# Attention feeding two expert stages: 128 partitions hold two token groups of one head instead of two heads

## The chip, the cores and the metric

The kernel runs on one core of one Trainium2 chip. The metric is the device time of one execution in microseconds. Engines are called as in the profile: PE (TensorE, with its weight loads as PEld), ACT (ScalarE), DVE (VectorE), POOL (GpSimd) and SP (SyncE), which issues the DMAs here.

## What is computed

```python
kv = np.einsum('bhsd,bhse->bhde', k, v)          # batch 4, heads 8, tokens 576, head size 64
out = np.einsum('bhsd,bhde->bhse', q, kv)
rms = np.sqrt(np.mean(out * out, axis=-1, keepdims=True) + 1e-06)
x = (out / rms * g_norm)                          # regrouped to 2304 tokens x 512
h = x @ w_in                                      # first expert stage, d_ff 2048
x = (h * np.clip(h + 3.0, 0.0, 6.0) / 6.0) @ w_out
p = domain_probs / (domain_probs.sum(-1, keepdims=True) + 1e-09)
for e in range(4):                                # second expert stage, 1024 wide each
    out += p[:, e:e + 1] * (np.maximum(x @ w1[e], 0.0) @ w2[e])
```

All inputs and the output are float32.

## The kernel before

The program has three stages: linear attention, a feed-forward stage in five units of hidden tiles, and the second expert stage in quads. Only the first is rebuilt by the change, and two small places that follow its token order.

**Head groups.** Attention is worked off in eight head groups i = 0 to 7: batch i // 2, four of the eight heads (HH = 4). The 576 tokens of a head are split as s * 9 + j, with s = 0 to 63 (CP) and j = 0 to 8 (CJ). In SBUF a tile of q, k or v is [128, NP, CJ, D] with NP = 2: partition x * 64 + s, head 2 * r + x. So the two partition halves hold two heads, and a matmul over tokens contracts 64 rows.

**Loads.** `att_load` (line 176) issues one DMA for each of q, k and v. Each writes 128 partitions, in contiguous runs of 9 x 64 floats. The tiles come from six buffers used in turn, so q, k, v of group i + 2 go where those of group i were. All DMAs stand in SP's queue in program order as the scheduler placed it; SP holds the queue while its next DMA waits for a buffer, and each DMA also waits for the landing of the eighth DMA before it (eight semaphores in turn).

**One group on the engines.** The orders of PE, ACT and DVE are written out by hand from line 483 on. For each i: `att_out(i)` multiplies the transposed q with the group's k^T v and squares the result for the norm; `att_q(i + 1)` transposes the next q on PE (line 214 for eight tokens of nine, line 216 for the ninth) and returns the copies to SBUF; `att_rms(i)` computes the scale; `att_kv(i + 1)` (line 225) accumulates k^T v of the next group; then two products of the feed-forward stage's first unit (`ff_mm`, lines 343 to 345), the transposes of the normed result of group i - 1 (`att_x`, line 308), and slices of the conversion of feed-forward weights (`conv`). PE takes them strictly in this order, so `att_kv` holds it until k and v of the next group have landed.

**k^T v before.** The product writes `kvp`, 64 x 64 for each head, two heads above one another:

```python
for j in range(CJ):
    for x in range(2):
        for r in range(NP):
            nc.tensor.matmul(
                kvp[half[x ^ r], r, :D], lhsT=t["k"][half[x], r, j, :], rhs=t["v"][half[x], r, j, :], ...)
```

That is 36 matmuls a group, each with 64 rows and 64 columns. Four neighbours use the four combinations of row half and column half. An f32 matmul leaves two records in the trace, so a group shows 72.

Of the kernel before, what the change touches and what calls it, by code (L numbers as in the profile page):

```python
# [17 lines left out]
def kernel(  # L18
# [18 lines left out]
    nc = tc.nc  # L37
# [136 lines left out]
    natile = [0]  # L174

    def att_load(i):
        b, hf = divmod(i, 2)
        t = {}
        for nm, src in (("q", q), ("k", k), ("v", v)):
            m = natile[0] % 6  # L180
            natile[0] += 1
            pool, tag = (accp, "acc") if m < 5 else (wp, f"w{m - 1}")
            t[nm] = pool.tile([P, NP, CJ, D], F32, tag=tag, name=f"{nm}in")
            nc.sync.dma_start(
                out=t[nm].rearrange("p r j d -> p r (j d)"),
                in_=src[b, hf * HH:(hf + 1) * HH].rearrange("(r x) (s j) d -> (x s) r (j d)", x=2, j=CJ),
            )
        st[i] = t


    half = [slice(x * D, (x + 1) * D) for x in range(2)]
    identx = ident.rearrange("p (x s) -> p x s", x=2)
    GB = TB // D
# [9 lines left out]
    def att_q(i):  # L203

        t = st[i]
        qT = wp.tile([P, (CJ + 1) * P], F32, tag=f"w{i % 2}", name="qT")
        t["qm"] = qm = qT[:, :2 * TB].rearrange("p (r x j s) -> p r x j s", r=NP, x=2, j=CJ // 2)
        t["q8"] = q8 = qT[:D, 2 * TB:].rearrange("p (r x s) -> p r x s", r=NP, x=2)
        pq = [pool.tile([P, 2, CJ // 2, CP], F32, tag=tag, name="pq") for pool, tag in ((psx, "x"), (psa, "a1"))]
        t["kvp"] = kvp = psk.tile([P, NP, TB], F32, tag="k", name="kvp")  # L210
        p8 = kvp[:D, :, D:D + P].rearrange("p r (x s) -> p r x s", x=2)
        for r in range(NP):
            for j in range(CJ // 2):
                nc.tensor.transpose(  # L214
                    pq[r][:, :, j, :], t["q"][:, r, 2 * j:2 * j + 2, :].rearrange("p j d -> p (j d)"), identx)
            nc.tensor.transpose(p8[:, r], t["q"][:, r, CJ - 1, :], identx)
        return [
            lambda r=r: nc.scalar.activation(
                out=qm[:, r].rearrange("p x j s -> p (x j s)"), in_=pq[r].rearrange("p x j s -> p (x j s)"),
                func=AF.Copy)  # L220
            for r in range(NP)] + [
            lambda: nc.scalar.activation(
                out=q8.rearrange("p r x s -> p r (x s)"), in_=kvp[:D, :, D:D + P], func=AF.Copy)]

    def att_kv(i):


        t = st[i]
        kvp = t["kvp"]
        for j in range(CJ):  # L230
            for x in range(2):
                for r in range(NP):
                    nc.tensor.matmul(  # L233
                        kvp[half[x ^ r], r, :D], lhsT=t["k"][half[x], r, j, :], rhs=t["v"][half[x], r, j, :],
                        start=(j == 0), stop=(j == CJ - 1))
        nc.scalar.activation(out=kvd[i % 2][:, 0], in_=kvp[:, :, :D], func=AF.Copy)
        for y in range(2):
            nc.scalar.activation(out=kvd[i % 2][half[y], 1], in_=kvp[half[1 - y], :, :D], func=AF.Copy)
# [3 lines left out]
    def att_out(i):  # L242

        t = st[i]
        kv = kvd[i % 2]
        for jj in range(CJ // 4):
            for r in range(NP):
                for x in range(2):
                    for y, c in ((0, 0), (1, 1), (0, 1), (1, 0)):
                        g = (2 * y + jj) * HH + 2 * r + x  # L250
                        nc.tensor.matmul(
                            group(g)[half[c]], lhsT=t["qm"][half[y], r, x, 2 * jj + c, :],
                            rhs=kv[half[y], x ^ r ^ y, r], start=True, stop=True)
        for x in range(2):
            for r in range(NP):
                g = 2 * GA + x
                nc.tensor.matmul(
                    group(g)[half[r]], lhsT=t["q8"][:, r, x, :], rhs=kv[half[0], x ^ r, r],
                    start=True, stop=True)
# [223 lines left out]
    with tc.manual_schedule(engines=engines):  # L483
# [97 lines left out]
        for y in range(2):  # L581
            h = half[y]
            for jp in range(2):
                j = slice(2 * y + jp, CJ - 1, 4)
                nc.vector.tensor_tensor(
                    out=prob[h, :B * HH].rearrange("p (b a) e -> p b a e", b=B)[:, :, 2 * jp:2 * jp + 2],
                    in0=dp[h, :, j], in1=psum_e[h, :, j].unsqueeze(3).to_broadcast([D, B, 2, E]), op=ALU.mult)
            nc.vector.tensor_tensor(
                out=prob[h, B * HH:], in0=dp[h, y::2, CJ - 1],
                in1=psum_e[h, y::2, CJ - 1:].to_broadcast([D, 2, E]), op=ALU.mult)  # L590

# [149 lines left out]
    def finish(p, e, i, ps):  # L741
# [10 lines left out]
        if e == E - 1:  # L752
            for y in range(2):
                if n < B * HH:
                    b, a = divmod(n, HH)
                    j = 4 * (a % 2) + a // 2 + 2 * y
                else:
                    b, j = 2 * (n - B * HH) + y, CJ - 1
                nc.sync.dma_start(
# [140 lines left out]
```

## Time and profile before

| | us |
|---|---|
| median of 3 runs | 1217.32 |
| lowest, highest | 1217.02, 1217.51 |
| the profiled execution | 1218.32 |
| its span, first to last instruction | 1216.5 |

The profile is that of one execution. Its page gives each engine's busy time, the DMA queues, and the chain of work that ended last. The trace behind it can be cut into stretches, and it says for each wait what ended it. In this profile attention lies in the first 74 us; the feed-forward stage and the second expert stage fill the rest, with PE busy almost throughout. [...]

### The profile page before, as it was taken

What the parts mean: (1) busy time and instruction counts of PE and PEld (TensorE: products, weight loads), DVE (VectorE), ACT (ScalarE), POOL (GpSimd) and SP (SyncE); (2) the same over time, 40 slices, a digit from 0 to 9 for tenths busy, and PEclk for the clock granted to TensorE, in tenths of its full rate; (3) what the DMA queues carried; (4) which work ended last, traced back from release to release, by engine and by line L of the source; (5) the groups of instructions that cost most, each with busy time, mean ns of one, the idle gap of its engine ahead of it and who ended that gap; (6) DMA issues with size and microseconds to landing.
All of it is one profiled execution on the core that took longest, in us unless ns stands there. A gap on an engine that the chain in (4) does not pass through costs nothing.

```text
span 1216.5 us, 17419 instructions
## 1 busy us (share of the span) xinstructions
PE 1195.3 (98%) x6999; PEld 1053.8 (87%) x6999; DVE 770.1 (63%) x1455; ACT 581.7 (48%) x1116; POOL 8.9 (1%) x16
## 2 busy tenths in 40 slices
PE   7899999999999999999999999999999999999997
PEld 6787888888888889999999989999999899999996
DVE  5889999953633844565656585656565856565652
ACT  5766554622322434444444554444445644444441
POOL 2000000000000000000000000000000000000000
PEclk9999999999999999999999999999999999999999
DMA  9612222300200002121111131122221422222202
GB/s 354 223 36 70 87 87 70 95 10 1 70 1 1 1 20 84 70 70 69 69 61 61 62 113 70 70 70 70 70 70 70 121 70 70 70 70 70 70 1 52
DMA packets 59345, 87.18 MB, mean 72 GB/s; under 512 B 3712, under 2 KB 36480, under 8 KB 59264
## 3 DMA queue, kind: packets, MB, share of 16 engines
q1 hardware_dynamic: 59264, 86.07, 21.1%
q8 instruction: 55, 0.90, 0.3%
q14 instruction: 26, 0.21, 0.0%
HBM read 81.34 MB, written 4.72 MB: 71 GB/s over the span
## 4 chain that ended last, share of the span: by engine, by line
PE 93%; DVE 3%; DMA 2%; ACT 1%; issue 1%; SPq 0%; DVEq 0%; ACTq 0%
PE po L734 32%; PE po L378 15%; PE qa L767 14%; PE qb L767 14%; PE ph L343 5%; PE ph L344 5%; PE ph L345 5%; DMA vin<-in_v_dram 1%; DMA qin<-in_q_dram 1%; DVE acc L750 1%; DVE xl L301 1%; PE kvp L233 1%; DVE r L357 0%; PE pq L214 0%; DVE ssq L264 0%
## 5 line engine op out<-in xcount | busy, mean ns | idle before, releaser
L734 PE MATMUL po<-wout,g 128*128 128x512 f32 x1728 | 402.1, 390 | 0.0
L734 PEld LDWEIGHTS po<-wout,g 128*128 128x128 f32 x1728 | 323.6, 188 | 65.4
L767 PE MATMUL qb<-xs,win 128*128 128x384 f32 x1008 | 203.5, 336 | 1.2 <-ACT us L808 1.2
L767 PE MATMUL qa<-xs,win 128*128 128x384 f32 x1008 | 203.1, 336 | 0.0
L378 PE MATMUL po<-gH,w 128*128 128x512 f32 (+1 forms) x632 | 191.8, 368 | 0.0
L767 PEld LDWEIGHTS qb<-xs,win 128*128 128x128 f32 x1008 | 178.1, 188 | 3.8 <-ACT us L808 1.8
L767 PEld LDWEIGHTS qa<-xs,win 128*128 128x128 f32 x1008 | 178.3, 188 | 2.2 <-ACT us L808 0.2
L641 DVE TENSOR_TENSOR wout<-raw,wout 128x512 fp32r<-128x512 f32 x96 | 62.2, 688 | 171.4 <-ACT wout L640 171.4
L640 ACT ACTIVATE wout<-raw 128x512 fp32r<-128x512 f32 x96 | 55.4, 625 | 227.0 <-PE po L734 227.0
L378 PEld LDWEIGHTS po<-gH,w 128*128 128x128 f32 x632 | 115.7, 188 | 20.5 <-ACT acc L392 0.6
L343 PE MATMUL ph<-xh,w 128*128 128x512 f32 (+1 forms) x320 | 119.2, 373 | 1.2 <-DVE r L357 1.2
L344 PE MATMUL ph<-xl,w 128*128 128x512 f32 (+1 forms) x320 | 118.4, 370 | 0.0
L345 PE MATMUL ph<-xh,w 128*128 128x512 f32 (+1 forms) x320 | 118.2, 370 | 0.0
L356 ACT ACTIVATE r<-ph,three 128x512 f32<-128x512 f32 (+1 forms) x80 | 51.6, 645 | 138.3 <-PE ph L345 138.2
L378 PE MATMUL po<-gL,w 128*128 128x512 f32 (+1 forms) x316 | 116.3, 368 | 0.0
L357 DVE SCALAR_TENSOR_TENSOR r<-r,ph 128x512 f32<-128x512 f32 (+1 forms) x80 | 50.5, 631 | 91.0 <-ACT r L356 90.8
L797 DVE SCALAR_TENSOR_TENSOR g<-sums,g 128x384 fp32r<-128x384 f32 x96 | 53.6, 559 | 81.4 <-ACT g L794 81.4
L794 ACT ACTIVATE g<-cs 128x384 fp32r<-128x384 f32 x96 | 50.4, 525 | 63.3 <-DVE cs L810 54.4
L640 ACT ACTIVATE win<-sums 128x512 fp32r<-128x512 f32 x96 | 60.6, 632 | 40.1 <-DVE sums L653 37.6
L343 PEld LDWEIGHTS ph<-xh,w 128*128 128x128 f32 x320 | 60.6, 189 | 12.4 <-DVE r L357 1.6
L797 DVE SCALAR_TENSOR_TENSOR g<-cs,g 128x384 fp32r<-128x384 f32 x96 | 53.2, 554 | 27.2 <-ACT g L794 27.2
L345 PEld LDWEIGHTS ph<-xh,w 128*128 128x128 f32 x320 | 60.6, 189 | 10.3
(129 smaller groups left out, 1260.7 us busy)
## 6 DMA issues: line engine op xcount, KB each, us to landing
raw<-in_moe_w_dram SPq DMA_DIRECT2D x96, 512.0 KB, 4.1
raw<-in_moe_w_in_dram SPq DMA_DIRECT2D x16, 512.0 KB, 3.7
raw<-in_moe_w_out_dram SPq DMA_DIRECT2D x16, 512.0 KB, 3.5
qin<-in_q_dram SPq DMA_DIRECT2D x8, 576.0 KB, 7.1
kin<-in_k_dram SPq DMA_DIRECT2D x8, 576.0 KB, 8.3
vin<-in_v_dram SPq DMA_DIRECT2D x8, 576.0 KB, 9.4
out_dram<-acc SPq DMA_DIRECT2D x36, 128.0 KB, 2.3
dp<-in_moe_domain_probs_dram SPq DMA_DIRECT2D x2, 36.0 KB, 8.4
```

Source lines behind the costliest of these rows:

```text
L343: nc.tensor.matmul(ph, lhsT=w[:, 0, c, :], rhs=xH[t][:, c, :], start=(c == 0), stop=False)
L344: nc.tensor.matmul(ph, lhsT=w[:, 0, c, :], rhs=xL[t][:, c, :], start=False, stop=False)
L345: nc.tensor.matmul(ph, lhsT=w[:, 1, c, :], rhs=xH[t][:, c, :], start=False, stop=(c == KD - 1))
L356: lambda: nc.scalar.activation(out=r, in_=ph, func=AF.Relu, bias=three[:, 0:1]),
L357: lambda: nc.vector.scalar_tensor_tensor(out=r, in0=r, scalar=6.0, in1=ph, op0=ALU.min, op1=ALU.mult),
L378: nc.tensor.matmul(po_t[u, t][o], lhsT=lhsT, rhs=rhs, start=(f == 0 and m == 0), stop=(f == UF[u] - 1 and m == 2))
L640: nc.scalar.activation(out=dst[0], in_=src, func=AF.Copy)
L641: nc.vector.tensor_tensor(out=dst[1], in0=src, in1=dst[0].bitcast(F32), op=ALU.subtract)
L734: nc.tensor.matmul(ps[i], lhsT=lhsT, rhs=w[:, f, y], start=(j == 0 and f == 0 and m == 0), stop=(j == FP - 1 and f == 1 and m == 2))
L767: nc.tensor.matmul(bank, lhsT=w[:, wy, AOP[m], c], rhs=xs[m][:, xy, c], start=first and n == 0, stop=n == 5, skip_group_check=True)
L794: nc.scalar.activation(out=g[f][:, 0, t], in_=src, func=func)
L797: nc.vector.scalar_tensor_tensor(out=g[f][:, 1, t], in0=src, scalar=0.0, in1=g[f][:, 0, t].bitcast(F32), op0=ALU.max, op1=ALU.subtract)
```

## The change

The partition halves hold two groups of tokens of the same head instead of two heads. A tile of q, k or v becomes [128, HH, JG, D] with JG = 5: half y holds tokens j = 5 * y to 5 * y + 4; the second half has four, so the fifth place stays empty there. Each tile is loaded by two DMAs, one for each partition half: 64 partitions with runs of 5 x 64 floats, and 64 partitions with runs of 4 x 64.

k^T v contracts 128 rows for four of the five places and 64 for the fifth: 20 matmuls a group in place of 36. The transposes of q take one head at a time, and those of the ninth token become four of 64 x 64 in place of two of 128 x 64. The output product has the same number and shape of matmuls; its left operand is addressed differently and `kv` loses the swap of heads. Which token stands in which row of the result changes, so the row scales `prob` and the addresses of the output stores follow; their sizes and counts stay.

```diff
@@ -173,6 +173,10 @@
     st = {}
     natile = [0]
 
+    JG, JP = CJ // 2 + 1, CJ // 2
+
+    half = [slice(x * D, (x + 1) * D) for x in range(2)]
+
     def att_load(i):
         b, hf = divmod(i, 2)
         t = {}
@@ -180,16 +184,16 @@
             m = natile[0] % 6
             natile[0] += 1
             pool, tag = (accp, "acc") if m < 5 else (wp, f"w{m - 1}")
-            t[nm] = pool.tile([P, NP, CJ, D], F32, tag=tag, name=f"{nm}in")
-            nc.sync.dma_start(
-                out=t[nm].rearrange("p r j d -> p r (j d)"),
-                in_=src[b, hf * HH:(hf + 1) * HH].rearrange("(r x) (s j) d -> (x s) r (j d)", x=2, j=CJ),
-            )
+            t[nm] = pool.tile([P, HH, JG, D], F32, tag=tag, name=f"{nm}in")
+            for y in range(2):
+                j = slice(y * JG, min((y + 1) * JG, CJ))
+                nc.sync.dma_start(
+                    out=t[nm][half[y], :, :j.stop - j.start].rearrange("p h j d -> p h (j d)"),
+                    in_=src[b, hf * HH:(hf + 1) * HH].rearrange("h (s j) d -> s h j d", j=CJ)[:, :, j]
+                    .rearrange("s h j d -> s h (j d)"))
         st[i] = t
 
 
-    half = [slice(x * D, (x + 1) * D) for x in range(2)]
-    identx = ident.rearrange("p (x s) -> p x s", x=2)
     GB = TB // D
     ppA = psp.tile([P, TB], F32, name="ppA")
     ppB = psp.tile([P, 2 * TB], F32, name="ppB")
@@ -204,35 +208,37 @@
 
         t = st[i]
         qT = wp.tile([P, (CJ + 1) * P], F32, tag=f"w{i % 2}", name="qT")
-        t["qm"] = qm = qT[:, :2 * TB].rearrange("p (r x j s) -> p r x j s", r=NP, x=2, j=CJ // 2)
-        t["q8"] = q8 = qT[:D, 2 * TB:].rearrange("p (r x s) -> p r x s", r=NP, x=2)
-        pq = [pool.tile([P, 2, CJ // 2, CP], F32, tag=tag, name="pq") for pool, tag in ((psx, "x"), (psa, "a1"))]
+        t["qm"] = qm = qT[:, :2 * TB].rearrange("p (h j t) -> p h j t", h=HH, j=JP // 2)
+        t["q8"] = q8 = qT[:D, 2 * TB:].rearrange("p (h s) -> p h s", h=HH)
+        pq = [pool.tile([P, 2, JP // 2, P], F32, tag=tag, name="pq") for pool, tag in ((psx, "x"), (psa, "a1"))]
         t["kvp"] = kvp = psk.tile([P, NP, TB], F32, tag="k", name="kvp")
         p8 = kvp[:D, :, D:D + P].rearrange("p r (x s) -> p r x s", x=2)
-        for r in range(NP):
-            for j in range(CJ // 2):
+        for h in range(HH):
+            r, x = divmod(h, 2)
+            for j in range(JP // 2):
                 nc.tensor.transpose(
-                    pq[r][:, :, j, :], t["q"][:, r, 2 * j:2 * j + 2, :].rearrange("p j d -> p (j d)"), identx)
-            nc.tensor.transpose(p8[:, r], t["q"][:, r, CJ - 1, :], identx)
+                    pq[r][:, x, j, :], t["q"][:, h, 2 * j:2 * j + 2, :].rearrange("p j d -> p (j d)"), ident)
+            nc.tensor.transpose(p8[:, r, x], t["q"][half[0], h, JP, :], ident[half[0], :D])
         return [
             lambda r=r: nc.scalar.activation(
-                out=qm[:, r].rearrange("p x j s -> p (x j s)"), in_=pq[r].rearrange("p x j s -> p (x j s)"),
-                func=AF.Copy)
+                out=qm[:, 2 * r:2 * r + 2].rearrange("p x j t -> p (x j t)"),
+                in_=pq[r].rearrange("p x j t -> p (x j t)"), func=AF.Copy)
             for r in range(NP)] + [
             lambda: nc.scalar.activation(
-                out=q8.rearrange("p r x s -> p r (x s)"), in_=kvp[:D, :, D:D + P], func=AF.Copy)]
+                out=q8.rearrange("p (r x) s -> p r (x s)", x=2), in_=kvp[:D, :, D:D + P], func=AF.Copy)]
 
     def att_kv(i):
 
 
         t = st[i]
         kvp = t["kvp"]
-        for j in range(CJ):
-            for x in range(2):
-                for r in range(NP):
+        for j in range(JG):
+            rows = slice(0, P) if j < JP else half[0]
+            for r in range(NP):
+                for x in range(2):
                     nc.tensor.matmul(
-                        kvp[half[x ^ r], r, :D], lhsT=t["k"][half[x], r, j, :], rhs=t["v"][half[x], r, j, :],
-                        start=(j == 0), stop=(j == CJ - 1))
+                        kvp[half[x], r, :D], lhsT=t["k"][rows, 2 * r + x, j, :], rhs=t["v"][rows, 2 * r + x, j, :],
+                        start=(j == 0), stop=(j == JP))
         nc.scalar.activation(out=kvd[i % 2][:, 0], in_=kvp[:, :, :D], func=AF.Copy)
         for y in range(2):
             nc.scalar.activation(out=kvd[i % 2][half[y], 1], in_=kvp[half[1 - y], :, :D], func=AF.Copy)
@@ -243,19 +249,18 @@
 
         t = st[i]
         kv = kvd[i % 2]
-        for jj in range(CJ // 4):
+        for jj in range(JP // 2):
             for r in range(NP):
                 for x in range(2):
                     for y, c in ((0, 0), (1, 1), (0, 1), (1, 0)):
-                        g = (2 * y + jj) * HH + 2 * r + x
                         nc.tensor.matmul(
-                            group(g)[half[c]], lhsT=t["qm"][half[y], r, x, 2 * jj + c, :],
-                            rhs=kv[half[y], x ^ r ^ y, r], start=True, stop=True)
+                            group((2 * y + jj) * HH + 2 * r + x)[half[c]],
+                            lhsT=t["qm"][half[y], 2 * r + x, jj, half[c]],
+                            rhs=kv[half[y], x ^ y, r], start=True, stop=True)
         for x in range(2):
             for r in range(NP):
-                g = 2 * GA + x
                 nc.tensor.matmul(
-                    group(g)[half[r]], lhsT=t["q8"][:, r, x, :], rhs=kv[half[0], x ^ r, r],
+                    group(2 * GA + x)[half[r]], lhsT=t["q8"][:, 2 * r + x, :], rhs=kv[half[0], x, r],
                     start=True, stop=True)
         t["xt"] = xt = wp.tile([P, NG, D], F32, tag=f"w{2 + i % 2}", name="xt")
         for pt, a, b in PIECES:
@@ -581,13 +586,13 @@
         for y in range(2):
             h = half[y]
             for jp in range(2):
-                j = slice(2 * y + jp, CJ - 1, 4)
+                j = slice(JG * y + jp, JG * y + JP, 2)
                 nc.vector.tensor_tensor(
-                    out=prob[h, :B * HH].rearrange("p (b a) e -> p b a e", b=B)[:, :, 2 * jp:2 * jp + 2],
+                    out=prob[h, :B * HH].rearrange("p (b z a) e -> p b z a e", b=B, z=2)[:, :, jp],
                     in0=dp[h, :, j], in1=psum_e[h, :, j].unsqueeze(3).to_broadcast([D, B, 2, E]), op=ALU.mult)
             nc.vector.tensor_tensor(
-                out=prob[h, B * HH:], in0=dp[h, y::2, CJ - 1],
-                in1=psum_e[h, y::2, CJ - 1:].to_broadcast([D, 2, E]), op=ALU.mult)
+                out=prob[h, B * HH:], in0=dp[h, y::2, JP],
+                in1=psum_e[h, y::2, JP:JP + 1].to_broadcast([D, 2, E]), op=ALU.mult)
 
     N3 = start[NU1 - 1, 0] + 3 * UF[NU1 - 1]
     for n in range(NB, N3 + 1):
@@ -753,9 +758,9 @@
             for y in range(2):
                 if n < B * HH:
                     b, a = divmod(n, HH)
-                    j = 4 * (a % 2) + a // 2 + 2 * y
+                    j = 2 * (a % 2) + a // 2 + JG * y
                 else:
-                    b, j = 2 * (n - B * HH) + y, CJ - 1
+                    b, j = 2 * (n - B * HH) + y, JP
                 nc.sync.dma_start(
                     out=out.rearrange("(b s j) d -> b j s d", b=B, j=CJ)[b, j], in_=acc2[i][half[y]])
```

On SP's queue, the loads of the sixth head group and what follows. Names are tile<-tensor; behind the name stand partitions and elements; the brackets say for what the row waits (DMAHW: a landing). Before:

```order
L184 DMA qin<-in_q_dram 128x2x576 [waits DMAHW5_49,PE_49]
L126 DMA raw<-in_moe_w_in_dram 128x4x256 [waits DMAHW6_49,DVE_49,Activation_49]
L184 DMA kin<-in_k_dram 128x2x576 [waits DMAHW7_49,PE_49]
L184 DMA vin<-in_v_dram 128x2x576 [waits DMAHW0_49]
L499 DMA dp<-in_moe_domain_probs_dram 64x4x36 [waits DMAHW1_49]
L499 DMA dp<-in_moe_domain_probs_dram 64x4x36 [waits DMAHW2_49]
L184 DMA qin<-in_q_dram 128x2x576 [waits DMAHW3_49,PE_49]
L184 DMA kin<-in_k_dram 128x2x576 [waits DMAHW4_49,PE_49]
```

After:

```order
L190 DMA qin<-in_q_dram 64x4x320 [waits DMAHW4_49,PE_49]
L190 DMA qin<-in_q_dram 64x4x256 [waits DMAHW5_49]
L190 DMA kin<-in_k_dram 64x4x320 [waits DMAHW6_49,PE_49]
L190 DMA kin<-in_k_dram 64x4x256 [waits DMAHW7_49]
L190 DMA vin<-in_v_dram 64x4x320 [waits DMAHW0_49]
L190 DMA vin<-in_v_dram 64x4x256 [waits DMAHW1_49]
L126 DMA raw<-in_moe_w_in_dram 128x4x256 [waits DMAHW2_49,DVE_49,Activation_49]
L190 DMA qin<-in_q_dram 64x4x320 [waits DMAHW3_49,PE_49]
L190 DMA qin<-in_q_dram 64x4x256 [waits DMAHW4_49]
L190 DMA kin<-in_k_dram 64x4x320 [waits DMAHW5_49,PE_49]
L190 DMA kin<-in_k_dram 64x4x256 [waits DMAHW6_49]
```

Each load has become two, the third w_in weight load has moved from ahead of the group's k to behind its v, and the two small loads of `dp` are gone from here: they now stand behind the last v.

On PE, from the end of the first group's output product to the second group's k^T v (pq and the part of kvp are the targets of q's transposes). Before:

```order
L214 MATMUL pq<-ident,qin 128x2x64 [waits DMAHW4_49]
L214 MATMUL pq<-ident,qin 128x2x64 x3
L216 MATMUL kvp<-ident,qin 64x128 [waits PE_49]
L214 MATMUL pq<-ident,qin 128x2x64 x4
L216 MATMUL kvp<-ident,qin 64x128
L233 MATMUL kvp<-vin,kin 64x64 [waits DMAHW6_49,DMAHW5_49]
L233 MATMUL kvp<-vin,kin 64x64 x35
```

After:

```order
L219 MATMUL pq<-ident,qin 128x128 [waits DMAHW7_49,DMAHW0_49]
L219 MATMUL pq<-ident,qin 128x128
L221 MATMUL kvp<-ident,qin 64x64 [waits PE_49]
L219 MATMUL pq<-ident,qin 128x128 x2
L221 MATMUL kvp<-ident,qin 64x64
L219 MATMUL pq<-ident,qin 128x128 x2
L221 MATMUL kvp<-ident,qin 64x64
L219 MATMUL pq<-ident,qin 128x128 x2
L221 MATMUL kvp<-ident,qin 64x64
L239 MATMUL kvp<-vin,kin 64x64 [waits DMAHW3_49,DMAHW4_49,DMAHW2_49,DMAHW1_49]
L239 MATMUL kvp<-vin,kin 64x64 x19
```

The ninth token's transposes are four in place of two and stand between pairs of the others. k^T v is 20 matmuls in place of 36, and its first one waits for four landings in place of two. The orders on ACT, DVE and POOL are the same as before.

## Rows read from the trace of the kernel before

**Rows 1.** Head of the page, and its instruction queue: packets, MB, share.

```profile
span 1216.5 us, 17419 instructions
...
PE 1195.3 (98%) x6999; PEld 1053.8 (87%) x6999; DVE 770.1 (63%) x1455; ACT 581.7 (48%) x1116; POOL 8.9 (1%) x16
...
q8 instruction: 55, 0.90, 0.3%
```

**Rows 2.** Stretches: length, busy of PE, PEld, DVE, ACT, POOL; clock, DMA share, GB/s.

```profile
4.00:30.00 26.00, 20.10 (x502) 16.26 (x501) 15.23 (x33) 15.60 (x36) 5.08 (x4) 1.00 1.03 387
...
40.00:62.00 22.00, 20.85 (x458) 17.25 (x461) 17.14 (x36) 16.40 (x39) 2.56 (x2) 0.92 0.54 167
62.00:78.00 16.00, 15.48 (x216) 13.08 (x216) 14.23 (x30) 12.18 (x27) 0.00 (x0) 1.00 0.01 2
...
36.00:46.00 10.00, 7.11 (x156) 5.86 (x156) 5.63 (x13) 5.50 (x13) 0.00 (x0) 0.83 0.79 241
```

**Rows 3.** The chain that ended last, its first part: start us, us, what.

```profile
2.75 8.18 DMA qin<-in_q_dram
10.95 10.83 DMA vin<-in_v_dram
21.91 1.31 PE kvp L233 x72
...
26.30 1.92 issue
...
30.03 1.21 PE kvp L233 x72
...
36.67 1.01 PE kvp L233 x57
37.68 2.89 issue
...
41.85 0.43 PE ph L344
...
49.60 0.24 PE ph L344
...
61.94 1.21 PE kvp L233 x72
...
73.91 1.39 PE po L546 x6
...
92.73 0.70 ACT x L145
```

**Rows 4.** SP's timeline, the last k and v load: start us, us, what.

```profile
49.23 0.37 SPq L184 DMA_DIRECT2D kin<-in_k_dram  x1
49.65 0.46 SPq L184 DMA_DIRECT2D vin<-in_v_dram  x1
```

**Rows 5.** DMA issues of the page: count, KB each, median us to landing.

```profile
vin<-in_v_dram SPq DMA_DIRECT2D x8, 576.0 KB, 9.4
out_dram<-acc SPq DMA_DIRECT2D x36, 128.0 KB, 2.3
```

**Rows 6.** Stretches with output stores (first two) and with loads of expert weights (third).

```profile
709.80:717.50 7.70, 7.12 (x38) 6.47 (x37) 7.63 (x16) 4.29 (x9) 0.00 (x0) 1.00 0.87 203
...
1207.60:1215.30 7.70, 1.41 (x7) 0.83 (x5) 2.20 (x4) 0.00 (x0) 0.00 (x0) 0.76 0.87 203
481.00:484.40 3.40, 3.40 (x21) 3.40 (x20) 2.15 (x5) 2.16 (x6) 0.00 (x0) 1.00 0.87 311
```

**Rows 7.** Matmuls on k and q: xcount, busy us, mean ns, idle before.

```profile
L233 PE MATMUL kvp<-vin,kin 64*64 64x64 f32 x576 | 10.6, 222 | 6.5 <-DMA vin<-in_v_dram 3.6 <-issue 2.9
...
L216 PE MATMUL kvp<-ident,qin 128*64 128x128 f32 x16 | 4.6, 287 | 0.3 <-DVE xl L301 0.2
```

**Rows 8.** What SP's queue waited for: us in total, times, longest us.

```profile
SPq L184 <- PE kvp L216: 13.8, 4, 5.9
SPq L184 <- PE kvp L233: 7.9, 5, 4.0
```

## The prediction

> **What bounds the kernel now.** I first read the head of the page: TensorE is busy for 1195.3 of 1216.5 us [rows 1], so nearly the whole span is the two mixture-of-experts stages, which the change doesn't touch except for a row order in the output. What can move lies in the attention stage. So I next cut the start of the span into stretches [rows 2]. From 4 to 30 us the DMA engines are busy all the time (share 1.03) at 387 GB/s; from 40 to 62 us their share is 0.54; from 62 us it is 0.01. The reader should see two halves there: the first is fed as fast as the queue delivers, the second isn't. Third I read the chain of waits [rows 3]. It begins with a q load that was issued at 2.75 us and landed 8.18 us later, goes on through the v load of the third head group (issued at 10.95, landed at 21.78), and reaches that group's k^T v product at 21.91. After that no load stands in the chain. It has two waits marked "issue", 1.92 us at 26.30 and 2.89 us at 37.68, where TensorE waits for nothing that the profile shows. The last k^T v product, of the eighth group, starts at 61.94, and the first matmul of the feed-forward stage's rest at 73.91. The last v load was issued at 49.65 us [rows 4], long before its product.
>
> So the question is how much slower the loads may become before they set the time again, and how much slower they do become.
>
> **The loads.** Each q, k or v load moves 576 KB (589,824 bytes) [rows 5]. Today one DMA writes it to 128 partitions in rows of 2,304 bytes. After the change two DMAs write 64 partitions each, with rows of 1,280 and 1,024 bytes. No large load to 64 partitions stands in this trace. The nearest rows are the output stores, which move 128 KB each [rows 5] from 64 partitions: of three bursts of twelve the first and the last run at 203 GB/s with the engines 0.87 busy [rows 6]. Their rows have 2,048 bytes. The weight loads of the second expert stage, with rows of 1,024 and 2,048 bytes on 128 partitions, have the same share of 0.87 and reach 311 GB/s [rows 6]. So it isn't the short rows that make the stores slow, and the engines aren't idle during them: their packets take longer. What sets the stores apart is the 64 partitions, and the direction. I take the partitions for the cause, because the share is that of a transfer that is held up and not of one that isn't asked for.
>
> That bounds a load after the change. The slow end is 203 GB/s, 2.91 us. If the gaps of the bursts were filled it would be 203/0.87 = 233 GB/s, 2.53 us. I take the middle, 218 GB/s and 2.71 us, because loads stand close in the queue (share 1.03) but closer packets also meet each other more often. The other bound, were the direction the cause, is 311/0.87 = 357 GB/s, 1.65 us. Today it is 589,824/387 GB/s = 1.52 us.
>
> [...]
>
> **The sum.** The queue works in order. The q load that landed at 10.93 us is its fifth entry, behind three other attention loads and one of 512 KB of weights; the five are 4 x 0.590 + 0.524 = 2.88 MB, or 7.4 us at 387 GB/s, so the queue flows from 10.93 - 7.4 = 3.5 us on. Before the last v load is done it has to move 24 attention loads (14.16 MB) and, in either order, five weight loads of 512 KB (2.62 MB, 6.8 us at 387 GB/s).
> - Before: 3.5 + 14.16 MB/387 + 6.8 = 3.5 + 36.6 + 6.8 = 46.9 us. The last product starts at 61.94, so 15.0 us are spare.
> - After: 3.5 + 14.16 MB/218 + 6.8 = 3.5 + 64.9 + 6.8 = 75.2 us. That is 13.3 us after 61.94.
> - At 203 GB/s: 3.5 + 69.7 + 6.8 = 80.0, 18.1 us later. At 233: 3.5 + 60.8 + 6.8 = 71.1, 9.2 us later.
>
> The loads use up the spare time from about 14.16 MB/(61.9 - 3.5 - 6.8 us) = 274 GB/s. What follows the last product (its copies, the last output product, the norm, the transposes) is one chain on TensorE, ACT and DVE, from 61.94 to 73.91, in the same order as before, so it shifts by the same amount. The second weight half of the third tile is issued behind the last v load; its first reader stands at 92.73 [rows 3] and shifts as well, so nothing waits for it.
>
> The profiled execution took 1218.32 us, its span and 1.8 us around it, 1.0 us above the median of 1217.32. I add the shift to the median: 1217.3 + 13.3 = **1230.6 us**; the profiled execution would become 1231.6.
>
> **The other parts.** The k^T v product goes from 72 records a group to 40 (each f32 matmul leaves two). A group takes 1.21 us, 17 ns a record [rows 3, 7]. Today four records run side by side, one in each quarter of the array; 128 tokens fill both row halves, so two run side by side. By records it would be 40 x 17 ns = 0.67 us, a gain of 0.54; by quarters 20 pairs at 1.21/18 = 67 ns, 1.34 us, a loss of 0.13. I take the loss, since the records overlap (222 ns each at 17 ns distance). Eight groups make between -4.3 and +1.0 us of TensorE time; while each group waits for its v, only the last group's share counts, within 0.6 us either way. The four 64-token transposes in place of two 128-token ones (287 ns a record, overlapping [rows 7]) come to nothing for the same reason. Orders on ACT, DVE and POOL are the same, and copies keep their sizes.
>
> SP issues 24 more DMAs at 0.37 to 0.46 us [rows 4], about 10 us of its time. They cost nothing while a half load occupies the wire for over 1.2 us. Each issue waits for the landing of the eighth DMA before it, now four loads instead of eight. SP waits 13.8 and 7.9 us for TensorE to free q and k buffers [rows 8], and everything behind in the queue waits along. Four loads are 10.8 us of wire, so the queue shouldn't run dry. If it did, a gap costs up to the 2.3 us from issue to landing of an output store [rows 5]; I leave it inside the range.
>
> **Rivals.**
> 1. *The halves run at full rate* (direction was the cause). The last v load would be ready at 3.5 + 14.16 MB/357 + 6.8 = 50 us, out of the way. The third group's v comes 9 x 0.13 = 1.2 us later. Against that, TensorE's stream loses 60 records a group (32 matmuls and as many weight loads, less two transposes with their loads). [...] That makes 1217.3 + 1.2 - 4.8 - 1.2 = 1212.5, **faster**. It decides above 274 GB/s. Chance 0.13. [...]
> 2. *The halves overlap in part*, because some engines fall behind and work on the other half. Near 274 GB/s nothing is left of the loss: **1217**, chance 0.07. Between 274 and 233 GB/s: 1220 to 1226, chance 0.10. For it speaks that DMA engines needn't keep step; against it that the stores also alternate between the halves and still run at 203.
> 3. *The waits lower the clock.* TensorE waits for each v in turn; before, 2.89 us of idleness was followed by the half level, and 1.92 was not. A group now takes 3 x 2.71 = 8.1 us of loads for some 6.6 us of work (the products at 30.03 and 36.67 [rows 3]), so single waits may be long enough. If the last group is caught, its tail pays one or two times 1.2 us: **1232 to 1234**, with 203 GB/s up to 1238. Chance 0.12.
>
> **How the numbers follow.** The forecast has 0.58: 1230.6, by itself 1226.5 to 1235.4. Slower is 0.58 + 0.12 + 0.10 = 0.80; within 0.2% (2.4 us, about what a measurement of this kernel can tell from no change) 0.07; faster 0.13. To hold eight in ten the range leaves out the full-rate rival and reaches from the upper part of the second one to the third with 203 GB/s: 1216 to 1238.
>
> **What would show it.** In the profile of the changed kernel the first 75 us should have a DMA share near 1 at 200 to 240 GB/s; the chain should run through v loads up to the last group, whose product starts near 75 us; waits of TensorE for v should appear in most groups; the "issue" waits should be gone from the chain or hidden. From the last product to the first matmul of the next stage it should be 12 us, as before. I am wrong if the attention loads run above 274 GB/s, or if the last product starts before 66 us.

## The result, and the profile after the change

The changed kernel takes 1231.87 us (median of four runs, 1229.69 to 1233.41) against 1217.41 us for the kernel before: a ratio of 1.0114, with a 95% interval of 1.0096 to 1.0133. The forecast was 1230.6. The profiled execution took 1232.03 us, with a span of 1230.2, 13.7 us longer than before. The total is close to the sum, but terms of the sum are off in opposite directions. The experiments are mostly about two of them, the rate of the loads and the order of the transposes.

The head of the page, to be read against [rows 1]:

```profile
span 1230.2 us, 16980 instructions
...
PE 1206.5 (98%) x6759; PEld 1058.1 (86%) x6759; DVE 769.9 (63%) x1455; ACT 582.3 (47%) x1116; POOL 8.9 (1%) x16
...
q8 instruction: 53, 0.87, 0.3%
```

TensorE has 240 matmul records fewer, the instruction queue moved two packets fewer, and the span is longer all the same. The stretches, as in [rows 2] (length; busy of PE, PEld, DVE, ACT, POOL; clock, which is the share of full speed that TensorE was granted; share of all sixteen DMA engines; GB/s):

```profile
4.00:30.00 26.00, 19.86 (x275) 13.53 (x274) 10.33 (x23) 11.37 (x25) 4.88 (x4) 0.87 1.09 247
30.00:50.00 20.00, 15.76 (x274) 12.18 (x274) 13.90 (x32) 11.92 (x28) 0.18 (x1) 0.91 1.10 249
50.00:70.00 20.00, 19.16 (x323) 15.29 (x324) 12.93 (x28) 12.49 (x30) 2.55 (x2) 0.91 1.10 253
70.00:78.00 8.00, 7.57 (x140) 5.88 (x139) 7.10 (x16) 6.68 (x16) 0.00 (x0) 1.00 0.39 89
```

The engines of the DMA are busy all the time up to 70 us, at 247 to 253 GB/s where [rows 2] has 387. The clock column is below 1 in three stretches: part of each ran at the half level (19.6 to 26.3 us, 33.2 to 36.5 and 50.3 to 53.6, each with a clock of 0.50). The last v load, from the instructions on the tile `vin` between 62 and 80 us (duration of one issue, first and last start; below it the times from issue to landing):

```profile
L190 SPq DMA_DIRECT2D vin<-in_v_dram x2: 596/676/755, 63.2 to 64.1; - x2
...
DMA to landing us min/median/max: 8.9/9.0/9.1
```

Its second half is issued at 64.1 and lands 9.1 us later, at 73.2. Now the chain that ended last, from 38 us on (start us, us, what):

```profile
38.64 11.39 DMA vin<-in_v_dram
...
50.17 2.57 PE kvp L239 x40
...
59.73 1.46 PE kvp L239 x40
...
67.56 1.46 PE kvp L239 x40
...
72.05 1.61 DVE xl L306 x3
...
73.70 0.24 PE kvp L221
73.94 0.37 PE pq L219 x2
74.31 0.17 PE kvp L221
74.49 0.37 PE pq L219 x2
74.86 0.17 PE kvp L221
75.03 0.37 PE pq L219 x2
75.40 0.17 PE kvp L221
75.57 1.46 PE kvp L239 x40
...
87.82 1.39 PE po L551 x6
```

Three things are to be seen. The last product starts at 75.57, close to the 75.2 of the sum, and the next stage's first matmul 12.25 us behind it, as before (11.97). But loads leave the chain at 50.03: the sixth, seventh and eighth group's products follow each other through compute alone, 7.83 and 8.01 us apart (and the sixth 9.56 behind the fifth, which ran at the half level). The last v had been there since 73.2; TensorE reached it 2.35 us late, because after the release of the ninth tokens' bank by DVE's `xl` (it ends at 73.66) four single transposes and six large ones stand ahead of the product, 1.87 us. Before, 0.85 us lay there: two ninth-token transposes and four large ones between 61.09 and 61.94.

So I formed this theory for the experiments: (a) the loads are slow because each DMA reaches one half of the partitions; had the last product followed its v at once, they would have cost 73.2 - 61.9 = 11.3 us; (b) the last 2 us come from TensorE's order of transposes, which the prediction had priced at nothing. The rivals: the loads are slow because of their short rows, their number, or the wait of each issue for the eighth landing before it; and the extra time of the groups comes from k^T v itself.

### The profile page after: what moved, and what is told of

The parts are those of the page before. It is cut to its first block, busy times and chain, and to the rows that moved or that the text cites. A ratio compares the mean times of both kernels' runs of the same rounds, so it can differ in the third digit from the quotient of the medians.

```text
span 1230.2 us, 16980 instructions
## 1 busy us (share of the span) xinstructions
PE 1206.5 (98%) x6759; PEld 1058.1 (86%) x6759; DVE 769.9 (63%) x1455; ACT 582.3 (47%) x1116; POOL 8.9 (1%) x16
## 2 busy tenths in 40 slices
DMA packets 65871, 87.15 MB, mean 71 GB/s; under 512 B 4096, under 2 KB 49152, under 8 KB 65792
## 4 chain that ended last, share of the span: by engine, by line
PE 92%; DMA 4%; DVE 2%; ACT 1%; issue 0%; SPq 0%; DVEq 0%
PE po L739 31%; PE po L383 15%; PE qa L772 14%; PE qb L772 14%; PE ph L348 5%; PE ph L349 5%; PE ph L350 5%; DMA vin<-in_v_dram 3%; DMA kin<-in_k_dram 1%; DVE acc L755 1%; PE kvp L239 1%; DVE xl L306 1%; PE pq L219 0%; DMA raw<-in_moe_w_out_dram 0%; DVE r L362 0%
```

## The experiments: results, and those on the loads

| kernel | median us | ratio to the kernel before (95%) |
|---|---|---|
| 1: before, loads cut into partition halves | 1234.65 | 1.0138 (1.0122 to 1.0155) |
| 2: before, loads cut by tokens | 1217.82 | 1.0000 (0.9990 to 1.0010) |
| 3: before, loads cut into even and odd partitions | 1218.23 | 1.0000 (0.9989 to 1.0011) |
| 4: changed kernel, upper halves from GpSimd's queue | 1235.78 | 1.0147 (1.0132 to 1.0162) |
| 5: changed kernel, tokens cut 512 + 64 | 1219.50 | 1.0020 (1.0010 to 1.0029) |
| 6: changed kernel, ninth transposes last | 1229.88 | 1.0097 (1.0079 to 1.0115) |
| 7: 5 and 6 together | 1215.67 | 0.9981 (0.9970 to 0.9992) |
| 8: before, ninth transposes last | 1217.64 | 1.0003 (0.9992 to 1.0014) |
| 9: 7, last tokens' product first | 1215.61 | 0.9985 (0.9976 to 0.9994) |
| 10: 9, output stores from 128 partitions | 1212.38 | 0.9956 (0.9944 to 0.9968) |

**Experiment 1.** Only the loads of the kernel before are cut.

```
-            nc.sync.dma_start(
-                out=t[nm].rearrange("p r j d -> p r (j d)"),
...
+            for y in range(2):
+                nc.sync.dma_start(
+                    out=t[nm][y * D:(y + 1) * D].rearrange("p r j d -> p r (j d)"),
+                    in_=src[b, hf * HH:(hf + 1) * HH].rearrange("(r x) (s j) d -> x s r (j d)", x=2, j=CJ)[y])
```

> The kernel before, with each q, k and v load cut in two by partition half (64 partitions each, the rows keep their 2,304 bytes); products and transposes are untouched. If writing 64 partitions at a time is what makes the loads slow, a tensor takes about 2.48 us (238 GB/s, what the changed kernel shows) in place of 1.52, the last v lands near 73 us in place of 47, the last product starts there in place of 61.94, and the time is 1217.4 + 11.3 = 1228.7 us. If the cause were short rows, these loads stay near 387 GB/s and the time stays at 1217.4. If the changed products or transposes were the cause, it also stays at 1217.4.

It took 1234.65 us. Neither the products nor the transposes have changed here, and the rows are as long as before, so the loss belongs to the cut of the loads; experiments 2 and 3 tell the halves from the number of DMAs. Two stretches of it:

```profile
4.00:30.00 26.00, 18.07 (x337) 13.99 (x336) 10.16 (x22) 11.08 (x25) 4.30 (x4) 0.80 1.06 250
...
62.00:70.00 8.00, 7.95 (x185) 6.66 (x179) 7.51 (x17) 6.57 (x17) 0.00 (x0) 1.00 0.76 205
```

The rate is that of the changed kernel (250 and 247 GB/s). In the trace's packet records a 2,304-byte packet takes 157 ns on the mean, 103 ns in the kernel before. But it is 6 us slower than I expected. From 62 us on the DMA share is 0.76: SP's queue is held up there. What it waited for in the first 75 us (us in total, times, longest):

```profile
SPq L185 <- PE kvp L216: 7.1, 3, 3.6
...
SPq L185 <- PE kvp L233: 3.5, 2, 3.3
```

10.6 us of its waits are for TensorE to free q and k buffers; in the changed kernel it is 2.8. The last product starts at 77.5. The chain has "issue" waits of 4.11, 1.54 and 2.54 us as well, which the changed kernel hasn't. That TensorE was late in freeing the buffers because of these is my reading, no run shows it apart.

**Experiment 2.** The DMAs of the changed kernel in number and row length, on the partitions of before.

```
+            for a, z in ((0, 5), (5, CJ)):
+                nc.sync.dma_start(
+                    out=t[nm][:, :, a:z],
+                    in_=src[b, hf * HH:(hf + 1) * HH].rearrange("(r x) (s j) d -> (x s) r j d", x=2, j=CJ)[:, :, a:z])
```

> The kernel before, with each load cut in two by tokens (0 to 4 and 5 to 8 of each partition): both DMAs write all 128 partitions, with rows of 1,280 and 1,024 bytes, so rows, number of DMAs and issues on SP are those of the changed kernel, the partitions those of before. If 64 partitions are the cause, the loads stay above the break-even of 274 GB/s (357 to 387) and the time within 1217 to 1218.5 us. If it is the short rows, the doubled number of DMAs or the wait of each issue for the eighth landing before it, the loads take about 2.48 us a tensor and the time is near 1229.

```profile
4.00:30.00 26.00, 21.05 (x548) 16.99 (x551) 15.79 (x33) 15.78 (x37) 5.09 (x4) 1.00 1.06 373
```

373 GB/s, and no change in time. In the packet records 1,280 bytes take 60 ns here and 90 in the changed kernel. Short rows, 24 more DMAs with their issues on SP and the window of eight landings cost nothing that can be measured.

**Experiment 3.** 64 partitions to a DMA again, every other one.

```
+            for y in range(2):
+                nc.sync.dma_start(
+                    out=t[nm][y::2].rearrange("p r j d -> p r (j d)"),
+                    in_=src[b, hf * HH:(hf + 1) * HH].rearrange("(r x) (s j) d -> (x s) r (j d)", x=2, j=CJ)[y::2])
```

> The kernel before, with each load cut in two by even and odd partitions in place of lower and upper half: again 64 partitions and rows of 2,304 bytes for each DMA, but spread over the whole partition range. [...] If it is the number of partitions of a DMA, whichever they are, packets stay near the 157 ns mean of the cut by halves and the time is near 1234.

1218.23 us, no change; packets of 2,304 bytes take 106 ns on the mean (median 93, as before).

```profile
4.00:30.00 26.00, 20.00 (x416) 16.18 (x415) 13.00 (x29) 13.79 (x33) 5.08 (x4) 0.88 0.95 335
```

So it isn't the number of partitions of a DMA but that all of them lie in one half. The rate is somewhat lower than in experiment 2 (335 GB/s) at a share below 1, but well above the break-even of 274.

**Experiment 4.** Both halves in flight at once.

```
-                nc.sync.dma_start(
+                (nc.sync, nc.gpsimd)[y].dma_start(
```

> The changed kernel, with the loads of the upper partition half issued by GpSimd on a queue of its own, so that both halves can be in flight at once. If each half by itself is the limit, both together come near the rate of before, no load ends the last groups, and what is left over the kernel before is the longer work of a group: 1218 to 1221 us. If the limit is one of the whole transfer (rows, packets), the time stays at 1230 to 1232. If the second queue is slow to be issued, it is slower still, and the gaps stand in the DMA share.

The first theory of this expectation fell: 1235.78 us, some 4 us above the changed kernel, where none of the three cases fits. In the packet records both queues move bytes in most stretches of 2 us up to 70 us, on the mean 89 GB/s on GpSimd's and 154 on SP's (which has the weights too), and together no more than one did:

```profile
50.00:62.00 12.00, 9.18 (x141) 6.94 (x139) 7.32 (x15) 6.76 (x15) 1.86 (x3) 0.86 1.08 241
```

The share is 1.08, so it isn't GpSimd's late issue. Why two queues, with packets for both halves at hand, move no more than one isn't to be seen: the records don't tell the partitions. The edit changes one thing more: GpSimd's packets have 4,096 bytes, where the same rows went in packets of 1,024. And the chain of this run has "issue" waits again, of 2.82 us and, at 63.36, of 0.88:

```profile
52.93 2.82 issue
```

Whether these make the 4 us isn't shown.

**Experiment 5.** The new k^T v and transposes with loads to 128 partitions. Partition p holds tokens 4p to 4p+3, and the last 64 tokens go to the lower 64 partitions by a DMA of 64 KB; the rows of `dp` and of the output follow, and `dp` is first set to 1, since its loads leave places open.

```
+            s0 = src[b, hf * HH:(hf + 1) * HH]
+            nc.sync.dma_start(
+                out=t[nm][:, :, :JP].rearrange("p h j d -> p h (j d)"),
+                in_=s0[:, :P * JP].rearrange("h (p j) d -> p h (j d)", j=JP))
+            nc.sync.dma_start(
+                out=t[nm][half[0], :, JP], in_=s0[:, P * JP:].rearrange("h s d -> s h d"))
```

> The changed kernel with another cut of the tokens: partition p holds tokens 4p to 4p+3 (one DMA to 128 partitions, rows of 1,024 bytes), and 64 partitions hold the last 64 tokens (rows of 256 bytes); transposes and products are those of the changed kernel, and the output rows follow. If 64 partitions are the cause, a tensor takes about 1.47 + 0.3 us, the last v lands near 54 us, before it is wanted, and the time shows the group's work alone: by my theory that work is 1 to 1.5 us longer than before in each group that no load hides (four single transposes between the large ones, 1.46 us for the product in place of 1.21), 1216 to 1222 us; by the full-rate rival of the prediction (the shorter instruction stream wins) 1212.5. If the loads aren't the cause, it stays at 1230 to 1232.

1219.50 us: by the ratios (1.0114 and 1.0020), some 11.5 of the 14 us that the change had cost are gone with the half-partition loads. The 256-byte packets take 18 ns, so the 64 KB are cheap. The last v lands at 55.7 us by the landing times of its trace, and the last product starts 6 us after it. What sets that start, from the chain:

```profile
53.63 1.46 PE kvp L239 x40
...
58.12 1.61 DVE xl L306 x3
...
59.77 0.24 PE kvp L221
60.01 0.37 PE pq L219 x2
60.38 0.17 PE kvp L221
60.55 0.37 PE pq L219 x2
60.92 0.17 PE kvp L221
61.10 0.37 PE pq L219 x2
61.47 0.17 PE kvp L221
61.64 0.90 PE kvp L239 x25
...
73.89 1.39 PE po L555 x6
```

With no load in the chain from 22.8 us on, products follow each other at 29.95, 37.78, 45.80, 53.63 and 61.64: 7.8 to 8.0 us apart, where the last groups of the kernel before needed 7.0 (from 47.95 over two groups to 61.94). From 25 us to the last product no "issue" wait over 0.1 us is left in this chain. So the full-rate rival was half right: the 4.8 us of "issue" waits of [rows 3] aren't in this chain, but four groups at 0.9 us more took most of that away, and the next stage's first matmul stands at 73.89, where it stood at 73.91. What this kernel takes longer than the one before lies behind that point. That the shorter stream removes the waits isn't shown: experiment 4 has the same stream and 3.7 us of them.

## Experiments on the order of the transposes

**Experiment 6.**

```
             for j in range(JP // 2):
                 nc.tensor.transpose(
                     pq[r][:, x, j, :], t["q"][:, h, 2 * j:2 * j + 2, :].rearrange("p j d -> p (j d)"), ident)
+        for h in range(HH):
+            r, x = divmod(h, 2)
             nc.tensor.transpose(p8[:, r, x], t["q"][half[0], h, JP, :], ident[half[0], :D])
```

> The changed kernel, with the four single ninth-token transposes of a group behind its eight large ones, not between them. In the changed kernel the last v lands at 73.2 us by the times of its queue and the last product starts 2.35 us later, because from the release of the ninth tokens' bank four single and six large transposes (1.87 us) stand ahead of it. By my theory the large ones now run ahead of the release and the last product follows its v: it starts near 73.5 and the time is 1231.9 - 2.2 = 1229.7 us. If the last product waits for loads alone (as the prediction's sum has it), or the large ones wait for the same release, the time stays at 1231.9.

1229.88 us, 2.0 less, where 1229.7 was expected. With four runs each this is not clear of noise (1.0097 with 1.0079 to 1.0115, against 1.0114 with 1.0096 to 1.0133), so the trace has to carry it. The end of the attention part in its chain:

```profile
62.07 9.41 DMA vin<-in_v_dram
...
71.62 0.42 PE kvp L241 x7
72.03 0.62 issue
72.66 1.35 PE kvp L241 x33
```

Now the last v is what ends last, and its product follows at once: 0.14 us behind the landing, where it was 2.35. This is the picture that the prediction had drawn; in the changed kernel itself it wasn't there. The product starts 3.95 us earlier than there; 2.2 us of that are the order, and the other 1.7 come from the last v, which landed at 71.48 in this run and at 73.22 in the other. Why it did isn't shown. The loads' own cost is about what is left, 1229.88 over this experiment's 1217.76 for the kernel before: some 12 us, with an "issue" wait of 0.62 us in it.

**Experiment 7.** The same edit on experiment 5.

> The cut of the tokens by 512 and 64 (loads to 128 partitions), with the ninth-token transposes behind the large ones. With that cut alone a group takes 7.97 us from product to product where the kernel before has 6.98, no load waits, and the time is 1219.5. If the transposes between release and product (1.87 us against 0.85) are what makes the group longer, a group falls to about 6.8 us, the last product starts near 57 us in place of 61.64, just behind the last v (55.5), and the time is 1214 to 1216 us, below both kernels. If the longer group comes from the product (1.46 against 1.21), or the large ones wait for the same release, it stays at 1218.5 to 1219.5.

```profile
56.74 1.19 PE pq L219 x8
57.93 0.34 PE kvp L223 x4
58.27 1.46 PE kvp L241 x40
```

1215.67 us, some 4 less than experiment 5 (the intervals of the two ratios lie apart) and below the kernel before. The four single transposes take 0.34 us in a row, 0.085 each; between pairs of large ones they took 0.17 to 0.24, and the pairs 0.37 instead of 0.30. The large ones no longer stand behind the release. The last product moves from 61.64 to 58.27. The work changes between 128-row and 64-row pieces twice in place of eight times, and takes 1.19 + 0.34 = 1.53 us in place of 4 x (0.17 + 0.37) = 2.16; that it is the changes which cost the difference isn't shown.

**Experiment 8.** The same order in the kernel before.

> The kernel before, with its two ninth-token transposes of a group behind the eight large ones. From release to product it has 0.30 + 0.44 + 0.11 = 0.85 us; if the four large ones (0.44) then run ahead of the release, about four groups that no load or issue wait hides get 0.44 us shorter and the time is 1215.5 us. If they wait for the same release, it stays at 1217.4.

1217.64 us, where 1215.5 had been expected: the interval leaves room for about 1 us, not for 2. TensorE's timeline before the last product:

```profile
59.57 1.26 PE L214 MATMUL pq<-ident,qin 128*128 128x128 f32 x8
60.67 0.38 PE L217 MATMUL kvp<-ident,qin 128*64 128x128 f32 x2
60.98 1.28 PE L234 MATMUL kvp<-vin,kin 64*64 64x64 f32 x72
```

The large transposes did move ahead of the release, and the last product stands at 60.98 in place of 61.87 (both from TensorE's timeline). But the chain of this kernel now runs over DVE and not over TensorE:

```profile
44.94 1.71 DVE xl L302 x3
...
51.41 1.58 DVE xl L302 x3
...
58.80 1.58 DVE xl L302 x3
...
65.14 1.59 DVE xl L302 x3
```

From `xl` to `xl` it is 6.5, 7.4 and 6.3 us, with DVE's and ACT's steps one behind the other between them. I read this as a floor, which the kernel before is near already (7.0): the changed kernel's order of transposes took a group to 7.9, above DVE's period, and regrouping brings it back to the floor, not below. No run made DVE's work shorter to show it.

**Experiment 9.** The four 64-row products of a group first, directly behind the 64-row transposes.

```
-        for j in range(JG):
+        for n, j in enumerate((JP, *range(JP))):
...
-                        start=(j == 0), stop=(j == JP))
+                        start=(n == 0), stop=(n == JP))
```

> The cut by 512 and 64 with the ninth-token transposes behind the large ones, and the four 64-row products of the last 64 tokens as the first of the group's k^T v in place of the last, so that they stand right behind the 64-row transposes. If each change between 64-row and 128-row work costs TensorE a tenth of a us or more, the product falls from 1.46 to 1.2 or 1.3 us and the time to 1215 us; if the length of the product comes from running two side by side only (20 pairs at 67 ns), it stays at 1.46 and the time at 1215.7.

```profile
58.18 0.34 PE kvp L223 x4
58.52 1.46 PE kvp L241 x40
```

1.46 us as before the edit, and no change in time: one change between 64-row and 128-row work fewer isn't seen here. The length goes with the 20 pairs of records, 73 ns each.

**Experiment 10.** The premise of the prediction was drawn from stores, not loads [rows 6]. With the tokens cut 512 + 64 both partition halves of an output tile go to evenly spaced rows, and one DMA can write them.

```
+            if n < B * HH:
+                b, a = divmod(n, HH)
+                j = 2 * (a % 2) + a // 2
+                nc.sync.dma_start(
+                    out=out[b * S:b * S + P * JP].rearrange("(p j) d -> j p d", j=JP)[j], in_=acc2[i])
...
```

> The same, with the output stores of the tiles that hold the first 512 tokens as one DMA from 128 partitions each (256 KB) in place of two from 64; with this cut of the tokens both halves go to evenly spaced rows. This is the premise of the prediction, tried on the stores themselves: were it the 64 partitions that hold them at 203 GB/s, a burst runs at 311 GB/s or more; the last burst (12 stores of 128 KB, 7.5 us, with nothing behind it) gets 2 to 3 us shorter and the time falls to 1212 to 1213.5 us. Were it the direction, the bursts stay at 203 GB/s and the time at 1215 to 1215.7 us.

The last burst of stores in experiment 9, which still stores by halves, and then in this one (columns as in [rows 6]):

```profile
1204.00:1212.00 8.00, 1.66 (x8) 1.04 (x6) 2.45 (x4) 0.00 (x0) 0.00 (x0) 0.74 0.85 197
```

```profile
1204.00:1209.50 5.50, 1.55 (x7) 0.94 (x5) 2.34 (x4) 0.00 (x0) 0.00 (x0) 1.00 0.84 273
```

273 GB/s at the same share, less than the 311 expected, but four of the eight DMAs of this burst still write from 64 partitions (the last 64 tokens' rows). The median 2,048-byte packet falls from 149 to 84 ns; packets of 140 ns and more, 594 of 768 in experiment 9, are 144 here. The time is 1212.38 us, 0.9956 of the kernel before (0.9944 to 0.9968), the fastest of all here. So the direction isn't the cause: stores too are slow by halves. For stores the number and size of the DMAs changed along with the half; for loads experiments 2 and 3 have told these apart.

## The prediction, point by point

**Total.** 1230.6 forecast, 1231.87 measured. That slow half loads set the time was right, but the rate isn't that of the forecast case. By the landing times an attention tensor took 2.37 us on the mean (67.1 us from the first tensor's landing to the last v's, less 12.5 for weights and two small loads, for 23 tensors), or 249 GB/s. That lies in the band of 233 to 274 for which the second rival had 1220 to 1226 us. In the sum alone this rate gives 3.5 + 14.16 MB/249 + 6.8 = 67.2 us for the last v and 1222.6 us for the kernel. The weights, 5.2 us longer than taken, and the 2.35 us between the last v and its product, taken at nothing, made up for it. That the total fits this closely is luck.

**Rate of the loads** (218 GB/s taken, 203 to 233 as bounds, full rate above 274): that the half of the partitions is the cause was right (experiments 1 to 3), the size was off. The changed kernel's queue moved at 247 to 253 GB/s with everything in it, above the upper bound. By its landing times the two halves of a tensor came 1.41 and 1.07 us after what was ahead of them in the middle of the stage, 2.48 us or 238 GB/s, later less, and 2.37 us on the mean, where 2.71 had been taken. The bound of 233 scaled the stores' packet time by their share; the loads run at a share of 1.09 to 1.10, which that step left out (203/0.87 x 1.09 would have been 254). That DMA engines needn't keep step, as the second rival had it, the landings show: the sixteen landing signals of one DMA stand up to 4.1 us apart in the kernel before and 3.9 in the changed one, in the first 80 us. Whether the loads, which alternate between the halves, ran above the 233 because engines work on both halves at once isn't shown.

**Weights in the queue** (6.8 us for five loads at 387 GB/s): mis-sized the other way. By the landing times the five came 1.41, 3.76, 1.34, 3.04 and 2.46 us after what was ahead of them, 12.0 us in all. They share the engines with the slow packets and slow down with them: a 4,096-byte packet of weights takes 191 ns in the median, 159 in the kernel before.

**Last v ready at 75.2**: it was 73.2. **Shift of 13.3 us**: 13.6, of which loads give 11.3. For the kernel before the same sum has 46.9 us, but in its trace the last v landed at 56.4, since the queue had also stood for buffers [rows 8]; the 15.0 us of spare time were those of the queue, and the last v had 5.4.

**Transposes at nothing**: this step failed. I priced four single transposes for two by their duration, and as hidden by the wait for v. The order of instructions that stands ahead of the prediction shows that six large ones fall behind the first single one, which waits for a release. They cost 1.87 - 0.85 = 1.0 us in each group whose v is there already, and the last group's v was. Experiment 7 puts the price at some 4 us where no load waits; for the changed kernel the trace of experiment 6 shows 2.2.

**k^T v**: 1.46 us against 1.21, a loss of 0.25 where 0.13 was taken. The choice of quarters rather than records was right (20 pairs, 73 ns each): the records of the last products start in fours 58 ns apart in the kernel before, and in pairs 58 ns apart in the changed one; the saving of matmul records saved no time.

**12 us behind the last product**: 12.25, of which 0.25 is the longer product.

**Issue waits**: gone from the chain, as one of the signs said, and it didn't matter, since loads filled that time; in experiment 5, where loads don't fill it, their absence is a gain. The full-rate rival's sum takes off 4.8 us for the two waits of [rows 3] (1.92 and 2.89 us), and 1.2 us that I had estimated for six matmuls at the half level after the longer one, from 0.43 in place of 0.24 us for each [rows 3]; no run shows that a shorter stream gains either. The kernel before shows 4.8 us of such waits and experiment 5 none, with a shorter stream, at 1219.50 us where the sum has 1212.5; experiment 4, with the same stream as the changed kernel, shows 3.7. So neither that the shorter stream removes them nor what TensorE waits for in them was shown.

**Lowered clock** (the third rival): it happened, not at the place feared. The stretches have a clock of 0.87 and 0.91, and the fifth group's product took 2.57 us at the half level in place of 1.46, right after a wait of 2.7 us for its v: 1.1 us more, where the rival takes 1.2 for such a stretch, from the same six matmuls. The last group ran at the full level. Without it the sixth product would have stood at 58.0 (50.17 + 7.83), the seventh at 66.4 (just behind its v, which landed at 66.2), and the last at 74.4, 1.2 us earlier than it did; that is worked out, no run has measured it. It isn't to be added to the price of the transposes: both stand in the 2.35 us between the last v and its product.

**SP's issue and window**: hidden, as said (experiment 2).

**The signs**: the last product near 75 us, the 12 us behind it and the missing "issue" waits came. The rate, 247 to 253 GB/s, is above the 200 to 240 named; the chain leaves the loads at the fifth group instead of the last; and TensorE waited for v before four groups of eight (9.0 us), not in most.

## What to carry to other kernels

Loads that fill a tile by two DMAs to the two partition halves ran at 250 GB/s here, where one DMA to 128 partitions ran at 387 (experiment 1); look for a cut of the data by which one DMA spans both halves (512 tokens as 4 to a partition, and the rest apart), before trading it for fewer matmuls, and look at the output stores too. A transpose that waited for a bank held all that stood behind it (1.87 us from release to product against 0.85): place such a one last in its group, and price the order, not the durations. A better order on one engine gained nothing where another's chain seems to be as long (the kernel before in experiment 8: 1217.64 us against 1217.41, with DVE's `xl` 6.3 to 7.4 us apart).

## What I had not expected

- DMAs to 64 partitions run at 335 GB/s if these are every other one, at 250 if they are one half (experiments 3 and 1); two queues with both halves in flight reach 241 (experiment 4).
- Weight loads to 128 partitions are slowed when they stand between half loads: their 4,096-byte packets take 191 ns in the median in the changed kernel in the first 80 us (226 on the mean), 159 in the kernel before (184).
- Four 64-row transposes take 0.34 us in a row and 0.75 between 128-row ones, which get longer as well (0.37 against 0.30 a pair).
